# Linear attention and a mixture of experts on one core: rows of the expert pairs gathered by quarters and turned by VectorE

## The chip, the cores and the metric

The kernel runs on one core of one Trainium2 chip. The metric is device time in microseconds, from the first to the last instruction of the launch with what lies around it; the time before is the median of three runs. Engines are TensorE (PE; its weight loads are listed as PEld), VectorE (DVE), ScalarE (ACT), GpSimd (POOL) and SyncE (SP), which issues most transfers.

## The reference

Eight batches of eight heads go through linear attention with exponential features; the result, 4608 rows of 512, goes through a mixture of eight experts, where each row goes to the one expert with the largest gate logit:

```python
def phi(x):
    proj = np.einsum('bhsd,df->bhsf', x, w_phi)
    proj = proj - np.max(np.abs(proj), axis=-1, keepdims=True)
    return np.concatenate([np.exp(proj), np.exp(-proj)], axis=-1)
...
expert_idx = np.argmax(logits, axis=1)
...
gate_w = probs[np.arange(N), expert_idx]
for e in range(E):
    mask = expert_idx == e
    xe = x[mask]
    h = np.maximum(xe @ w1[e], 0.0)
    ye = h @ w2[e]
    out[mask] = gate_w[mask, None] * ye
```

All products keep fp32 accuracy: an operand is split into a high part (rounded to fp32r) and a low part (the rest), and three products (high x high, high x low, low x high) are summed in PSUM.

## The kernel before

**Attention stage** (to about 400 us). Sixteen units of two heads for two batches each. Each unit projects q and k, builds features, sums k features against v, and divides; `normalize` makes rows `xrow`, and `store_rows` writes them to the DRAM table `x_dram`, 128 columns at a time, on SP's queue. A row of `x_dram` has 512 columns and 4 more, in which `gate_store` puts the gate of the row.

**Routing.** While the last attention units run, `route` finds each row's expert and its rank in it. `tokens_of` turns this, with 72 small matmuls into `pp`, into a table `gidx` of 44 blocks of 128 row numbers (gathers) and `sidx` (scatters); `experts_of` finds the expert of each block. Three blocks of the largest expert (`NLEAD`) are known earlier and gathered ahead.

**Expert stage.** Blocks 0 to 37 are worked in 19 pair units of two blocks of one expert (`NPAIR`), the rest as singles (units 19 to 21; more only behind a branch that this input does not take). For each block:
- `gather_rows` (L833) fetches 128 rows of 516 columns into `xg` (4 buffers) with one indirect DMA on GpSimd's queue;
- `x_parts` (L1014 to L1017) turns `xg` with four TensorE transposes into a PSUM tile `px` (2 buffers), ScalarE copies it to the high part `xh`, VectorE subtracts it to the low part `xl` (2 buffers each, a pair unit in one);
- `pair_first` (L1034 to L1042) makes 512 of the unit's hidden values for both blocks in 24 matmuls of 256 columns, four times per unit; ScalarE takes the relu into `hh`, VectorE the rest into `hl`;
- `pair_second` (L1054 to L1056) does twelve matmuls of 512 columns per step into two PSUM tiles `po`, which `write` (L1102, L1104) scales on ScalarE by the gate, column 512 of `xg`, and scatters to the output on GpSimd's queue.

**The order.** The pair loop is written out: per unit u four slots j, each with `pair_first(u, j)`, in slots 2 and 3 `x_parts` of unit u+1, then a `pair_second` step of the slot before; slot 0 calls `gather(u + 1)`, and each slot calls `weights` for two of the eight weight pieces of a later unit. `weights` (L989, L990) casts a raw piece to its high part `wh` on ScalarE and subtracts the low part `wl`, six pieces on VectorE and two (`POOL_LO`, pieces 3 and 7) on GpSimd; raw pieces come over SP's queue, only where the expert changes. This source order gives priorities; a planner then orders each engine's queue from its own estimates of when instructions are ready, within the buffers, and places the waits. `behind` puts an instruction behind another on the same engine.

Of the kernel before, what the change touches and what calls it, by code (L numbers as in the profile page):

```python
# [9 lines left out]
F32 = mybir.dt.float32  # L10
F32R = mybir.dt.float32r
BF16 = mybir.dt.bfloat16
I32 = mybir.dt.int32
# [6 lines left out]
P = 128  # L20
# [25 lines left out]
KD = DM // P  # L46
KF = FF // P
W = 73
XW = DM + 4

WARM = 7
BIG = 8192.0
# [3 lines left out]
def tile_linear_attention_moe(  # L56
# [21 lines left out]
    gidx = keep.tile([P, NB], I32, name="gidx")  # L78
    sidx = keep.tile([P, NB], I32, name="sidx")
    eidx = keep.tile([1, NB], I32, name="eidx")  # L80
    nblk = keep.tile([1, 1], I32, name="nblk")
    gidx0 = keep.tile([P, NLEAD], I32, name="gidx0")
    sidx0 = keep.tile([P, NLEAD], I32, name="sidx0")
# [44 lines left out]
    iota_em = const.tile([P, E], F32, name="iota_em")  # L128
    part_i = const.tile([P, 1], I32, name="part_i")
    part1 = const.tile([P, 1], F32, name="part1")  # L130
    hb_i = const.tile([P, NG, NC], I32, name="hb_i")
    hbase = const.tile([P, NTILE], F32, name="hbase")

# [7 lines left out]
    def constants2():  # L141

        G.memset(ltri, 1.0)
        G.affine_select(ltri, ltri, [[1, P]], ALU.is_gt, 0.0, base=0, channel_multiplier=-1)

        G.iota(iota_i, [[1, P]], base=0, channel_multiplier=0)
        G.tensor_copy(iota_p, iota_i)
        G.tensor_scalar_add(iota_em, iota_e, -float(E))
        G.iota(part_i, [[0, 1]], base=1, channel_multiplier=1)
        G.tensor_copy(part1, part_i)  # L150


        G.iota(hb_i[:, :, 0:4], [[18, NG], [2, 4]], base=0, channel_multiplier=0)
        G.iota(hb_i[:, :, 4:8], [[18, NG], [2, 4]], base=9, channel_multiplier=0)
        G.iota(hb_i[0:64, :, 8:9], [[18, NG], [0, 1]], base=8, channel_multiplier=0)
        G.iota(hb_i[64:P, :, 8:9], [[18, NG], [0, 1]], base=16, channel_multiplier=0)
        G.tensor_copy(hbase, hb_i.rearrange("p g c -> p (g c)"))
        G.tensor_scalar_mul(hbase, hbase, 64.0)
# [8 lines left out]
    bases = [rt.tile([P, E], BF16, name="base0")]  # L167
    V.memset(bases[0], 0.0)

    x_dram = dram.tile([NT, XW], F32, name="x_dram")  # L170


    NPC = KD + KF // 2
# [33 lines left out]
    def col(c):  # L207
        return (0 if c == 8 else P * (c + 1))

    def store_rows(g, t, w0, n, c0=0, nc_=NC, eng=nc.sync):  # L210

        for bb in range(2):
            t0 = (2 * g + bb) * S
            lo, hi = max(c0, 4 * bb), min(c0 + nc_, 4 * bb + 4)
            if lo < hi:
                r0 = t0 + (lo - 4 * bb) * P
                eng.dma_start(
                    x_dram[r0 : r0 + (hi - lo) * P, w0 : w0 + n].rearrange("(c p) w -> p c w", p=P),
                    t[:, lo - c0 : hi - c0, :],
                )  # L220
            if c0 + nc_ == NC:
                nc.sync.dma_start(
                    x_dram[t0 + 4 * P : t0 + S, w0 : w0 + n], t[64 * bb : 64 * bb + 64, 8 - c0, :]
                )

    def load(st, x, part):
# [177 lines left out]
    def num_steps(st, chunks):  # L404


        def step(c, hh, s):
            i = 2 * c + hh
            part = [a <= i < b for a, b in PARTS].index(True)
            a, b = PARTS[part]  # L410
            if (i, s) == (a, 0):
                st["pn"] = ps_nm.tile([P, 7, W], F32, name="pn")
            pn = st["pn"]
            qp, s0 = st["qp", c]
            m = T.matmul(  # L415
                pn[:, i - a, :] if c < 8 else pn[:, 2 + hh : 6 : 2, :],
                qp[:, s, s0 + hh, :],
                st["kf"][:, hh, s, c // 4, :] if c < 8 else st["kf"][:, hh, s],
                start=(s == 0),
                stop=(s == 1),  # L420
            )
            if (i, s) == (b - 1, 1):
                if c == 8:
                    A.copy(pn[D:P, 2:4, :], pn[D:P, 4:6, :])
                normalize(st, a, b, st["pr"])
                if c == 8:
                    lgc_done[st["g"]] += 1
                    eng = G if st["g"] == NG - 1 and st["pr"] == 2 else nc.sync
                    store_rows(st["g"], st["x"], st["pr"] * P, P, eng=eng)
# [194 lines left out]
    def route(g, lgc, c0, n, final=None):  # L624
# [122 lines left out]
            V.tensor_scalar_add(r["se"], r["se"], 1e-9)  # L747

        def gate_store():
            gt = sg.tile([P, NC, XW - DM], F32, name="gt", bufs=2)  # L750
            V.reciprocal(gt[:, 0:n], r["se"].unsqueeze(2).to_broadcast([P, n, XW - DM]))
            store_rows(g, gt, DM, XW - DM, c0, n)

        steps = [logits, top, shift, candidates, first_top, one_hot]
        ranks = [rank, rank_low, rank_high]
# [72 lines left out]

        return [pick_lead, find, find_rows, fetch]

    def gather_rows(index, rows):
        xg = xgp.tile([P, XW], F32, name="xg")
        G.indirect_dma_start(  # L833
            out=xg,
            out_offset=None,
            in_=x_dram[0:rows],
            in_offset=bass.IndirectOffsetOnAxis(ap=index, axis=0),
            bounds_check=rows - 1,
            oob_is_err=False,
        )  # L840
        return xg

    v_tiles = []
    for i in range(2):
# [80 lines left out]
    def tokens_of():  # L925

        pp = ps_kv.tile([P, NB], F32, name="pp", tag="pk")
        for j in range(NTILE):
            T.matmul(pp, sel_p[:, j, :], bsel[:, j, :], start=(j == 0), stop=False)
            T.matmul(pp, sel_h[:, j, :], bsel[:, j, :], start=False, stop=(j == NTILE - 1))  # L930
        V.tensor_scalar(gidx, pp, -1.0, 0.0, op0=ALU.add, op1=ALU.max)
        emp = sg.tile([P, NB], F32, name="emp")
        V.tensor_scalar(emp, pp, 0.5, BIG, op0=ALU.is_lt, op1=ALU.mult)
        st["places"] = V.scalar_tensor_tensor(sidx, pp, -1.0, emp, op0=ALU.add, op1=ALU.add)

    def experts_of():
        ends = sg.tile([1, 2, E], F32, name="ends")
        G.tensor_tensor(ends[:, 0], first[0:1], paired[0:1], op=ALU.add)
        G.tensor_tensor(ends[:, 1], start[0:1], singles[0:1], op=ALU.add)
        V.tensor_reduce(nblk, ends[:, 1], axis=AX.X, op=ALU.max)  # L940
        eg = sg.tile([1, 2, NB, E], F32, name="eg")
        places = ((first[0:1], ends[:, 0], 0, 2 * NPAIR), (start[0:1], ends[:, 1], 2 * NPAIR, NB))
        for low, high, n0, n1 in places:
            for j, edge in enumerate((low, high)):
                m = V.tensor_tensor(
                    eg[:, j, n0:n1],
                    iota_p[0:1, n0:n1].unsqueeze(2).to_broadcast([1, n1 - n0, E]),
                    edge.unsqueeze(1).to_broadcast([1, n1 - n0, E]),
                    op=ALU.is_ge,
                )  # L950
                behind(m, st["places"])
        G.tensor_tensor(eg[:, 0], eg[:, 0], eg[:, 1], op=ALU.subtract)
        G.tensor_tensor(eg[:, 0], eg[:, 0], iota_e[0:1].unsqueeze(1).to_broadcast([1, NB, E]), op=ALU.mult)
# [24 lines left out]
    def weights(u, k):  # L978
# [16 lines left out]
        if u > 0:  # L995
            load_weights(u + 1, k)

    def gather(u):
        if u >= lim[0]:
            return  # L1000
        for b in blocks(u):
            if ("xg", b) not in st:
                st["xg", b] = early_rows[b] if b < NLEAD else gather_rows(gidx[:, b : b + 1], NT)

    def x_parts(u, i):
        if u >= lim[0] or i >= len(blocks(u)) or ("x", u, i) in st:
            return
        if i == 0:
            st["x", u] = [mp.tile([P, KD, 2 * P], F32R, name=n) for n in ("xh", "xl")]
        st["x", u, i] = True  # L1010
        xg = st["xg", blocks(u)[i]]
        px = ps_x.tile([P, KD, P], F32, name="px")
        for k in range(KD):
            T.transpose(px[:, k, :], xg[:, k * P : (k + 1) * P], ident)  # L1014
        xh, xl = (x[:, :, i * P : (i + 1) * P] for x in st["x", u])
        A.copy(xh, px)
        V.tensor_tensor(xl, px, xh, op=ALU.subtract)  # L1017

# [156 lines left out]
    for u in range(1, NPAIR):  # L1175
        for j in range(4):
# [10 lines left out]
    gather(NPAIR + 1)  # L1187
    first_product(NPAIR, 0)
    pair_second(NPAIR - 1, 3)
    weights(NPAIR + 1, 2)  # L1190
# [6 lines left out]
    gather(NPAIR + 2)  # L1197

    def step(u):
        gather(u + 3)  # L1200
        first_product(u + 1, 0)
        h_parts(u, 0)
# [89 lines left out]
```

## Time and profile before

| | |
|---|---|
| median of 3 runs | 902.75 us (902.69 to 902.82) |
| profiled execution, its own time | 900.9 us |
| its span | 899.1 us |
| mean granted TensorE clock | 0.993 of full speed |
| HBM read / written | 128.42 / 20.26 MB |

The span is what the views of the trace cover; times in them are microseconds from its start. A group of the view by lines gives the engine, the operation, the shapes, its count, its busy time in us and the mean of one in ns, and then the idle time of the engine in front of it.

### The profile page before, as it was taken

How to read it: one execution, taken by the hardware profiler on the slowest of the kernel's cores; microseconds unless marked ns; L12 is line 12 of the kernel's file. 1: busy time of each engine (PE TensorE's matmuls, PEld its weight loads, DVE VectorE, ACT ScalarE, POOL GpSimd, SP SyncE). 2: the span in 40 equal slices, each digit the busy share in tenths (PEclk: the TensorE clock that was granted, in tenths of full speed). 3: DMA queues.
4: the chain of work that ended last, by engine and by line, in shares of the span. 5: the costliest groups of instructions: out<-in, count | busy, mean ns of one | idle time of the engine just before them, and what ended most of it. 6: DMA issues, size and time to landing. Idle time of an engine off the chain costs nothing. (4 is left out here: it accounts for less than half of the span.)

```text
span 899.1 us, 18045 instructions
## 1 busy us (share of the span) xinstructions
PE 875.6 (97%) x6767; PEld 825.2 (92%) x6767; DVE 564.6 (63%) x984; ACT 580.4 (65%) x886; POOL 463.0 (51%) x297
## 2 busy tenths in 40 slices
PE   6999999999999999999999999999999999999994
PEld 5999999999999999998899999999999999999883
DVE  6887878877887788759844445544555444444540
ACT  6988888888788888653755555555555555555651
POOL 6777766766677777641533333333333333333341
PEclk9999999999999999999999999999999999999998
DMA  5333333333343333261352243522434634346630
GB/s 158 94 105 100 98 91 93 105 110 109 110 110 100 108 110 80 80 209 19 98 173 71 95 164 118 163 73 77 139 113 146 218 113 146 116 153 223 222 122 15
DMA packets 66795, 106.65 MB, mean 119 GB/s; under 512 B 10830, under 2 KB 28750, under 8 KB 66704
## 3 DMA queue, kind: packets, MB, share of 16 engines
q1 hardware_dynamic: 59312, 84.50, 30.3%
q0 software_dynamic: 6720, 20.80, 7.4%
q8 instruction: 55, 0.90, 0.4%
q14 instruction: 36, 0.29, 0.1%
q10 hardware_dynamic: 672, 0.15, 0.1%
HBM read 128.42 MB, written 20.26 MB: 165 GB/s over the span
## 5 line engine op out<-in xcount | busy, mean ns | idle before, releaser
L990 DVE TENSOR_TENSOR wl<-raw,wh 128x1024 fp32r<-128x1024 f32 x126 | 161.7, 1288 | 144.8 <-ACT wh L989 144.8
L989 ACT CAST wh<-raw 128x1024 fp32r<-128x1024 f32 x168 | 175.1, 1049 | 100.0 <-PE po L1056 71.5
L990 POOL TENSOR_TENSOR wl<-raw,wh 128x1024 fp32r<-128x1024 f32 x42 | 101.4, 2415 | 176.0 <-ACT wh L989 175.7
L415 PE MATMUL pn<-kf,qp 128*128 128x73 f32 (+1 forms) x1152 | 185.0, 255 | 0.0
L1035 PE MATMUL pm<-xl,wh 128*128 128x256 f32 x608 | 172.3, 283 | 0.0
L1036 PE MATMUL pm<-xh,wl 128*128 128x256 f32 x608 | 172.2, 283 | 0.0
L415 PEld LDWEIGHTS pn<-kf,qp 128*128 128x128 f32 x1152 | 171.7, 190 | 0.1
L1034 PE MATMUL pm<-xh,wh 128*128 128x256 f32 x608 | 171.6, 282 | 0.0
L297 POOL TENSOR_TENSOR kl<-e,kh 128x1024 fp32r<-128x1024 f32 x47 | 112.4, 2391 | 102.7 <-ACT kh L295 73.7
L274 DVE TENSOR_REDUCE mx<-ps_proj 128x4 f32<-128x512 f32 (+1 forms) x160 | 101.3, 633 | 58.4 <-PE ps_proj L270 55.4
L1054 PE MATMUL po<-wh,hh 128*128 128x512 f32 x304 | 121.9, 401 | 0.0
L1055 PE MATMUL po<-wl,hh 128*128 128x512 f32 x304 | 119.4, 393 | 0.1
L1035 PEld LDWEIGHTS pm<-xl,wh 128*128 128x128 f32 x608 | 116.4, 191 | 3.0 <-DVE xl L1017 0.2
L1034 PEld LDWEIGHTS pm<-xh,wh 128*128 128x128 f32 x608 | 116.4, 191 | 2.9
L1056 PE MATMUL po<-wh,hl 128*128 128x512 f32 x304 | 118.4, 390 | 0.0
L1036 PEld LDWEIGHTS pm<-xh,wl 128*128 128x128 f32 x608 | 116.4, 191 | 0.0
L359 PE MATMUL pk<-kh,vl 128*64 128x256 f32 x320 | 107.9, 337 | 0.0
L359 PE MATMUL pk<-kh,vh 128*65 128x256 f32 x320 | 105.8, 331 | 1.5 <-ACT kvT L377 1.5
L359 PE MATMUL pk<-kl,vh 128*65 128x256 f32 x320 | 106.2, 332 | 0.8 <-DVE kl L297 0.8
L275 DVE TENSOR_TENSOR t<-ps_proj,mx 128x512 f32<-128x512 f32 (+1 forms) x160 | 101.5, 635 | 4.6
L240 POOL TENSOR_TENSOR xl<-xr,xh 128x512 fp32r<-128x512 f32 (+2 forms) x63 | 101.5, 1629 | 2.5 <-ACT xh L239 2.4
L1042 DVE SCALAR_TENSOR_TENSOR hl<-pm,hh 128x512 fp32r<-128x512 f32 x76 | 52.2, 687 | 69.0 <-ACT hh L1041 69.0
(206 smaller groups left out, 1875.0 us busy)
## 6 DMA issues: line engine op xcount, KB each, us to landing
raw<-w SPq DMA_DIRECT2D x168, 512.0 KB
vt<-vv SPq DMA_DIRECT2D x15, 640.0 KB
x_dram<-xrow SPq DMA_DIRECT2D x30, 256.0 KB
xr<-kT SPq DMA_DIRECT2D x15, 320.0 KB
xr<-qT SPq DMA_DIRECT2D x15, 320.0 KB
xr<-kT SPq DMA_DIRECT2D x17, 256.0 KB
xr<-qT SPq DMA_DIRECT2D x17, 256.0 KB
x_dram<-xrow SPq DMA_DIRECT2D x32, 32.0 KB
```

What stands on the lines that cost most here:

```text
L240: el.tensor_tensor(xl[:, 0:n], xr[:, 0:n], xh[:, 0:n], op=ALU.subtract)
L297: eng.tensor_tensor(kl, e[:, 0:m], kh, op=ALU.subtract)
L359: return T.matmul(st["pk", bb][0:n, hh, :], (vl if j == 1 else vh)[:, 2 * (c + (bb if c == 8 else 0)) + hh, 0:n], (kl if j == 2 else kh)[: ...
L415: m = T.matmul(pn[:, i - a, :] if c < 8 else pn[:, 2 + hh : 6 : 2, :], qp[:, s, s0 + hh, :], st["kf"][:, hh, s, c // 4, :] if c < 8 else s ...
L989: A.copy(th, raw[k])
L990: m = (G if k in (POOL_LO if u else POOL_LO0) else V).tensor_tensor(tl, raw[k], th, op=ALU.subtract)
L1034: T.matmul(pm[:, i], th, xh[:, k, :], start=(k == 0), stop=False)
L1035: T.matmul(pm[:, i], th, xl[:, k, :], start=False, stop=False)
L1036: T.matmul(pm[:, i], tl, xh[:, k, :], start=False, stop=(k == KD - 1))
L1054: T.matmul(po, hh[:, i, r], th[:, c], start=(i == j == 0), stop=False)
L1055: T.matmul(po, hh[:, i, r], tl[:, c], start=False, stop=False)
L1056: T.matmul(po, hl[:, i, r], th[:, c], start=False, stop=(i == 1 and j == 3))
```

## The change

- In units 4 to 18 (`by_quarters`) each block is fetched by four indirect DMAs. The table `x_dram` has rows of exactly 512 columns now and is read as 4 x 4608 quarter rows of 128 columns. DMA c puts, on partition 32q + t, quarter q of row 32c + t of the block. The quarter numbers, 4 x row + q, come from `quarters_of`: four fp32 matmuls spread the row numbers over the partitions, one VectorE instruction makes the integers `qidx`.
- Such a block is turned by one VectorE transpose of 32x32 squares into `px`, in place of four TensorE transposes. On partition p then lie columns 4p to 4p+3. The rows of w1 are put into that order on the host, and the transposes that stay on TensorE read every fourth column.
- Gates go to a table `g_dram` of 4 columns; `gather_gates` fetches them per block with an indirect DMA of their own into `gate` (6 buffers), and `write` scales by that.
- Rows are gathered two units ahead instead of one (`gather(u + 2)`); gates one unit ahead. `gather(2)` and the first gates stand before the loop, behind the arithmetic of `experts_of`.
- In units 1 to 18 VectorE does all eight low-part subtractions of the weights; in unit 0 and the singles GpSimd keeps two.

```diff
-XW = DM + 4
+XW = 4
+Q = P // 4
...
+        for q in range(4):
+            G.memset(quad[q * Q : (q + 1) * Q], float(q))
...
-    x_dram = dram.tile([NT, XW], F32, name="x_dram")
+    x_dram = dram.tile([NT, DM], F32, name="x_dram")
+    g_dram = dram.tile([NT, XW], F32, name="g_dram")
...
-            store_rows(g, gt, DM, XW - DM, c0, n)
+            store_rows(g, gt, g_dram, 0, XW, c0, n)
...
+    def gather_quarters(b):
+        xg = xgp.tile([P, 4, P], F32, name="xg")
+        quarters = x_dram.rearrange("t (q d) -> (t q) d", q=4)
+        for c in range(4):
+            behind(fetch_rows(xg[:, c, :], quarters, qidx[:, c, b : b + 1], 4 * NT), st["experts"])
+        return xg
+
+    def gather_gates(b):
+        gate = xgp.tile([P, XW], F32, name="gate", bufs=6)
+        index = gidx0[:, b : b + 1] if b < NLEAD else gidx[:, b : b + 1]
+        return gate, fetch_rows(gate, g_dram, index, NT)
...
+    def quarters_of():
+        spread = raw2.tile([P, 4, P], F32, name="spread")
+        G.tensor_copy(
+            spread.rearrange("p c (i t) -> p c i t", i=4),
+            ident.rearrange("p (c t) -> p c t", c=4).unsqueeze(2).to_broadcast([P, 4, 4, Q]),
+        )
+        pq = ps_kv.tile([P, 4, NB], F32, name="pq", tag="pk")
+        for c in range(4):
+            T.matmul(pq[:, c, :], spread[:, c], st["rows"], start=True, stop=True)
+        V.tensor_scalar(qidx, pq, 4.0, quad, op0=ALU.mult, op1=ALU.add)
...
-        m = (G if k in (POOL_LO if u else POOL_LO0) else V).tensor_tensor(tl, raw[k], th, op=ALU.subtract)
+        m = (G if k in (POOL_LO0 if u == 0 else POOL_LO if u >= NPAIR else ()) else V).tensor_tensor(tl, raw[k], th, op=ALU.subtract)
...
+    def by_quarters(u):
+        return 4 <= u < NPAIR
...
-        for k in range(KD):
-            T.transpose(px[:, k, :], xg[:, k * P : (k + 1) * P], ident)
         xh, xl = (x[:, :, i * P : (i + 1) * P] for x in st["x", u])
+        if by_quarters(u):
+            px = px.rearrange("p c (k t) -> p c k t", t=Q)
+            V.transpose(px, xg.rearrange("p c (d k) -> p c k d", k=KD))
+            px = px.rearrange("p c k t -> p k c t")
+            xh, xl = (x.rearrange("p k (c t) -> p k c t", t=Q) for x in (xh, xl))
+        else:
+            for k in range(KD):
+                T.transpose(px[:, k, :], xg.rearrange("p c d -> p (c d)")[:, k : DM : KD], ident)
...
-        A.activation(ob, po, AF.Copy, scale=st["xg", b][:, DM : DM + 1])
+        A.activation(ob, po, AF.Copy, scale=st["gate", b][:, 0:1])
...
     experts_of()
+    quarters_of()
+    gates(0)
+    gather(2)
+    gates(1)
...
             if j == 0:
-                gather(u + 1)
+                gather(u + 2)
+                gates(u + 1)
```

## Rows read from the trace of the kernel before

**Rows 1.** The page's table of engines: busy time, share of the span, instructions.
```profile
PE 875.6 (97%) x6767; PEld 825.2 (92%) x6767; DVE 564.6 (63%) x984; ACT 580.4 (65%) x886; POOL 463.0 (51%) x297
```

**Rows 2.** Windows of the pair loop: length, busy us by engine, clock, DMA, GB/s.
```profile
core 0: us, PE busy (x) PEld busy (x) DVE busy (x) ACT busy (x) POOL busy (x), PEclk, DMA share, GB/s
437.00:460.00 23.00, 23.00 (x152) 21.04 (x151) 17.06 (x16) 16.04 (x20) 9.37 (x5) 1.00 0.40 137
...
600.00:693.00 93.00, 93.00 (x607) 85.15 (x606) 44.67 (x49) 49.95 (x65) 36.17 (x24) 1.00 0.36 118
```

**Rows 3.** Timeline of PE, one pair unit: start, duration (us), instruction.
```profile
602.61 0.28 PE L1034 MATMUL pm<-xh,wh 128*128 128x256 f32 x1
...
605.48 0.60 PE L1014 MATMUL px<-ident,xg 128*128 128x128 f32 x4
...
608.67 0.28 PE L1034 MATMUL pm<-xh,wh 128*128 128x256 f32 x1
...
614.72 0.28 PE L1034 MATMUL pm<-xh,wh 128*128 128x256 f32 x1
...
620.34 0.28 PE L1034 MATMUL pm<-xh,wh 128*128 128x256 f32 x1
...
625.96 0.28 PE L1034 MATMUL pm<-xh,wh 128*128 128x256 f32 x1
```

**Rows 4.** Groups by line: transposes of the whole span; VectorE from 490 to 860 us.
```profile
L1014 PE MATMUL px<-ident,xg 128*128 128x128 f32 x164 | 24.6, 272 | 0.8 <-DMA xg<-x_dram,gidx 0.8
...
L990 DVE TENSOR_TENSOR wl<-raw,wh 128x1024 fp32r<-128x1024 f32 x97 | 122.2, 1261 | 128.2 <-ACT wh L989 128.2
...
L1017 DVE TENSOR_TENSOR xl<-px,xh 128x512 fp32r<-128x512 f32 x32 | 21.8, 681 | 0.0
```

**Rows 5.** Timeline of GpSimd, one pair unit; in brackets the idle time before.
```profile
504.06 1.02 POOL L1104 DMA_INDIRECT out<-ob,sidx  x1 [4.45 <-ACT ob L1102]
505.39 1.04 POOL L833 DMA_INDIRECT xg<-x_dram,gidx  x1 [0.30 <-issue]
...
508.06 1.03 POOL L1104 DMA_INDIRECT out<-ob,sidx  x1 [0.30 <-issue]
...
527.41 1.02 POOL L1104 DMA_INDIRECT out<-ob,sidx  x1 [4.46 <-ACT ob L1102]
```

**Rows 6.** Timelines of GpSimd and VectorE: two gathers beside subtractions.
```profile
433.53 2.01 POOL L833 DMA_INDIRECT xg<-x_dram,gidx  x1 [0.31 <-ACT wh L989]
...
600.15 1.01 POOL L833 DMA_INDIRECT xg<-x_dram,gidx  x1 [0.30 <-issue]
...
432.30 2.36 DVE L990 TENSOR_TENSOR wl<-raw,wh 128x1024 fp32r<-128x1024 f32 x2 [1.65 <-ACT wh L989]
...
600.31 1.23 DVE L990 TENSOR_TENSOR wl<-raw,wh 128x1024 fp32r<-128x1024 f32 x1 [0.18 <-ACT wh L989]
```

**Rows 7.** Groups by line and form, VectorE: a copy and a strided reduction.
```profile
L397 DVE COPY kf<-pf 128x292 f32<-128x292 f32 x32 | 14.5, 453 | 3.3 <-PE pf L386 3.3
...
L645 DVE TENSOR_REDUCE pt<-lgc 128x72 f32<-128x576 f32 x3 | 3.8, 1251 | 0.9 <-PE ps_proj L269 0.9
```

**Rows 8.** Timelines of ScalarE and VectorE around 611 us.
```profile
610.90 1.05 ACT L989 CAST wh<-raw 128x1024 fp32r<-128x1024 f32 x1 [0.98 <-PE pm L1035]
...
613.12 0.68 DVE L1042 SCALAR_TENSOR_TENSOR hl<-pm,hh 128x512 fp32r<-128x512 f32 x1
613.73 0.68 DVE L1017 TENSOR_TENSOR xl<-px,xh 128x512 fp32r<-128x512 f32 x1
```

**Rows 9.** Timelines before the pair loop, and one group by line.
```profile
428.65 0.65 PE L1014 MATMUL px<-ident,xg 128*128 128x128 f32 x4 [0.82 <-DMA xg<-x_dram,gidx]
...
428.45 0.92 POOL L953 TENSOR_TENSOR eg<-eg,iota_p 1x352 f32<-1x352 f32 x1
...
L386 PE MATMUL pf<-fold,kvT 65*128 65x73 f32 x256 | 40.5, 252 | 0.0
```

**Rows 10.** Instructions on the tile xg: transfer time, in us from issue.
```profile
DMA to landing us min/median/max: 3.5/3.6/3.7
```

More of the change, by code (lines that the diff above doesn't have):

```diff
@@ L80, in tile_linear_attention_moe @@
     eidx = keep.tile([1, NB], I32, name="eidx")
+    qidx = keep.tile([P, 4, NB], I32, name="qidx")
     nblk = keep.tile([1, 1], I32, name="nblk")
@@ L130, in tile_linear_attention_moe @@
     part1 = const.tile([P, 1], F32, name="part1")
+    quad = const.tile([P, 1], F32, name="quad")
     hb_i = const.tile([P, NG, NC], I32, name="hb_i")
@@ L208, in col, with store_rows @@
         return (0 if c == 8 else P * (c + 1))
-    def store_rows(g, t, w0, n, c0=0, nc_=NC, eng=nc.sync):
+    def store_rows(g, t, rows, w0, n, c0=0, nc_=NC, eng=nc.sync):
         for bb in range(2):
@@ L217, in store_rows @@
                 eng.dma_start(
-                    x_dram[r0 : r0 + (hi - lo) * P, w0 : w0 + n].rearrange("(c p) w -> p c w", p=P),
+                    rows[r0 : r0 + (hi - lo) * P, w0 : w0 + n].rearrange("(c p) w -> p c w", p=P),
                     t[:, lo - c0 : hi - c0, :],
@@ L222, in store_rows @@
                 nc.sync.dma_start(
-                    x_dram[t0 + 4 * P : t0 + S, w0 : w0 + n], t[64 * bb : 64 * bb + 64, 8 - c0, :]
+                    rows[t0 + 4 * P : t0 + S, w0 : w0 + n], t[64 * bb : 64 * bb + 64, 8 - c0, :]
                 )
@@ L428, in step @@
                     eng = G if st["g"] == NG - 1 and st["pr"] == 2 else nc.sync
-                    store_rows(st["g"], st["x"], st["pr"] * P, P, eng=eng)
+                    store_rows(st["g"], st["x"], x_dram, st["pr"] * P, P, eng=eng)
             return m
@@ L749, in gate_store @@
         def gate_store():
-            gt = sg.tile([P, NC, XW - DM], F32, name="gt", bufs=2)
-            V.reciprocal(gt[:, 0:n], r["se"].unsqueeze(2).to_broadcast([P, n, XW - DM]))
-            store_rows(g, gt, DM, XW - DM, c0, n)
+            gt = sg.tile([P, NC, XW], F32, name="gt", bufs=2)
+            V.reciprocal(gt[:, 0:n], r["se"].unsqueeze(2).to_broadcast([P, n, XW]))
+            store_rows(g, gt, g_dram, 0, XW, c0, n)
         steps = [logits, top, shift, candidates, first_top, one_hot]
@@ L829, in lead, with fetch_rows @@
         return [pick_lead, find, find_rows, fetch]
[L831 to L834, printed above, removed]
+    def fetch_rows(out, source, index, rows):
+        return G.indirect_dma_start(
+            out=out,
             out_offset=None,
-            in_=x_dram[0:rows],
+            in_=source[0:rows],
             in_offset=bass.IndirectOffsetOnAxis(ap=index, axis=0),
@@ L840, in gather_rows @@
         )
-        return xg
+    def gather_rows(index, rows):
+        xg = xgp.tile([P, 4, P], F32, name="xg")
+        fetch_rows(xg.rearrange("p q d -> p (q d)"), x_dram, index, rows)
+        return xg
+    def gather_quarters(b):
+        xg = xgp.tile([P, 4, P], F32, name="xg")
+        quarters = x_dram.rearrange("t (q d) -> (t q) d", q=4)
[6 more added lines that the diff above has]
+        return gate, fetch_rows(gate, g_dram, index, NT)
     v_tiles = []
@@ L934, in tokens_of @@
         st["places"] = V.scalar_tensor_tensor(sidx, pp, -1.0, emp, op0=ALU.add, op1=ALU.add)
+        st["rows"] = sg.tile([P, NB], F32, name="rows_f")
+        V.tensor_scalar(st["rows"], pp, -1.0, 0.0, op0=ALU.add, op1=ALU.max)
+    def quarters_of():
[6 more added lines that the diff above has]
+        for c in range(4):
+            T.matmul(
+                pq[:, c, :],
+                spread[:, c],
+                st["rows"],
+                start=True,
+                stop=True,
+            )
+        V.tensor_scalar(qidx, pq, 4.0, quad, op0=ALU.mult, op1=ALU.add)
     def experts_of():
@@ L952, in experts_of @@
         G.tensor_tensor(eg[:, 0], eg[:, 0], eg[:, 1], op=ALU.subtract)
-        G.tensor_tensor(eg[:, 0], eg[:, 0], iota_e[0:1].unsqueeze(1).to_broadcast([1, NB, E]), op=ALU.mult)
+        st["experts"] = G.tensor_tensor(eg[:, 0], eg[:, 0], iota_e[0:1].unsqueeze(1).to_broadcast([1, NB, E]), op=ALU.mult)
         with nc.allow_low_precision("experts are integers"):
@@ L1002, in gather, with gates @@
             if ("xg", b) not in st:
-                st["xg", b] = early_rows[b] if b < NLEAD else gather_rows(gidx[:, b : b + 1], NT)
+                if b < NLEAD:
+                    st["xg", b] = early_rows[b]
+                elif by_quarters(u):
+                    st["xg", b] = gather_quarters(b)
+                else:
+                    st["xg", b] = gather_rows(gidx[:, b : b + 1], NT)
+    def gates(u):
+        if u < lim[0]:
+            for b in blocks(u):
+                if ("gate", b) not in st:
+                    st["gate", b], m = gather_gates(b)
+                    behind(m, st["experts"])
     def x_parts(u, i):
@@ L1012, in x_parts @@
         px = ps_x.tile([P, KD, P], F32, name="px")
-        for k in range(KD):
-            T.transpose(px[:, k, :], xg[:, k * P : (k + 1) * P], ident)
         xh, xl = (x[:, :, i * P : (i + 1) * P] for x in st["x", u])
+        if by_quarters(u):
[3 more added lines that the diff above has]
+            xh, xl = (x.rearrange("p k (c t) -> p k c t", t=Q) for x in (xh, xl))
+        else:
+            for k in range(KD):
+                T.transpose(px[:, k, :], xg.rearrange("p c d -> p (c d)")[:, k : DM : KD], ident)
         A.copy(xh, px)
@@ L1182, in tile_linear_attention_moe @@
             if j == 0:
-                gather(u + 1)
+                gather(u + 2)
+                gates(u + 1)
             for du, k in AHEAD_W[j]:
                 weights(u + du, k)
-    gather(NPAIR + 1)
     first_product(NPAIR, 0)
@@ L1199, in step @@
     def step(u):
+        gates(u)
         gather(u + 3)
@@ L1259, in blocks, with shuffled @@
         return res
+    def shuffled(w):
+        return np.ascontiguousarray(w.reshape(E, P, KD, FF).transpose(0, 2, 1, 3).reshape(E, DM, FF))
     def rows(a):
@@ L1278 @@
         "w_gate": np.ascontiguousarray(inputs["moe_w_gate"]),
-        "w1": np.ascontiguousarray(inputs["moe_w1"]),
+        "w1": shuffled(np.asarray(inputs["moe_w1"])),
         "w2": np.ascontiguousarray(inputs["moe_w2"]),
```

## Prediction, made before the change was run

> **What bounds the kernel now.** I read the page's table of engines first, then the windows, then single timelines. TensorE is busy 97% of the span [rows 1]. The windows say where that share is a limit: from 437 us on, in the pair loop, PE is busy in every microsecond of each window, at a granted clock of 1.00 (the 2.4 GHz level), while VectorE has 44.67, ScalarE 49.95 and GpSimd 36.17 of 93 us [rows 2]. So in this stage a microsecond is won only by what leaves PE's queue, and the other engines may take on work until one of them is full or hands something over late.
>
> The PE timeline gives the length of one pair unit. Starts of the four first products of a unit: 602.61, 608.67, 614.72, 620.34, and the next unit at 625.96 [rows 3]. The two slots in which a block's rows are turned (four transposes each, the row at 605.48 is one set) last 6.06 and 6.05 us, the two without them 5.62 each: 23.35 us in all. The GpSimd timeline shows the same period, 504.06 to 527.41 [rows 5].
>
> **The removed transposes.** The blocks of units 4 to 18 are turned one unit earlier, in loop units 3 to 17: 15 units, 30 blocks, 120 of the 164 transposes. A slot without them is (6.06 + 6.05 − 2 × 5.62) / 2 = 0.435 us shorter. That is the price to use, not the 272 ns of one transpose [rows 4], which overlaps its neighbours. 30 × 0.435 = 13.1 us; a unit falls to 22.48 us. This is the first term: −13.1.
>
> **VectorE.** Per unit it works 44.67 / 93 × 23.35 = 11.2 us [rows 2]. The change adds two low-part subtractions that GpSimd did in the pair loop (1.26 us each [rows 4]) and two turns of 128x512. No row shows a turn. From below it is bounded by the copy of 292 columns, 0.45 us, from above by the strided reduction of 576 columns, 1.25 us [rows 7]; I take 0.7, near the 0.68 of xl, which moves the same 512 columns [rows 4]. Sum: 11.2 + 2.5 + 1.4 = 15.1 us of 22.48 (16.2 at 1.25). VectorE has the room, so the term is nothing as long as its results are in time; cover is 6 to 7 us a unit. The Trainium skill, "VectorE: DVE Perf Modes", section "The three transpose paths", gives 311 ns for a 128x128 bf16 turn on VectorE; four of them would be an estimate of 1.24 us, and the sum would be the same.
>
> **Is a turned block in time?** Today the order is tight: hl at 613.12 and xl at 613.73 for a unit whose first product starts at 614.72 [rows 3, 8]. If the turn stood in VectorE's queue behind hl, then turn 0.7, xh 0.58 and xl 0.68 would end near 613.81 + 1.96 = 615.8; without the transposes PE wants it at 614.72 − 0.435 + 0.12 = 614.4. But a turn needs nothing from PE, and the queues don't run in source order: two out scatters stand before the two gathers in the source, yet one scatter goes out behind them [rows 5]; and the cast at 610.90 starts exactly when PE's last read frees its buffer, about half a unit before its place in the source, ahead of the hh of the slot [rows 8]. Work is issued as early as buffers allow. The buffers (4 for xg, 2 for px, 2 for xh and xl) let a block be gathered two units and turned one unit before use. So I cost the new chain at nothing, with 1.4 us a unit as the other bound.
>
> **GpSimd.** A unit now has 8 quarter gathers, 2 gate gathers and 2 scatters instead of 2 gathers and 2 scatters, and loses two subtractions. Issues follow each other every 1.33 us [rows 5]: 12 × 1.33 = 16.0 of 22.48 us. One row warns: the gather at 433.53 took 2.01 us, begun inside a pair of VectorE subtractions that ran from 432.30 to 434.66; the one at 600.15, begun before the subtraction at 600.31, took 1.01 [rows 6]. So an issue that starts inside such a subtraction may wait for its end. Eight subtractions a unit can each hold up one issue by at most their own 1.26 us: 16.0 to 26.1 us; half of that wait gives 21.0, still under 22.48. A gather lands 3.6 us after issue [rows 10] and has more than a unit of lead. I take nothing. The Trainium skill, "SBUF — State Buffer", section "Who interferes with whom", says that a VectorE instruction with two SBUF inputs shuts out a GpSimd instruction that reads SBUF, whichever comes second waiting for the other's end. The trace agrees, with 2.01 against 1.01 us, and a rival below stands on that row.
>
> **The change-over to the pair loop.** Four fp32 matmuls build the quarter indices: by 40.5 us / 256 = 0.16 us of PE for a small fp32 matmul [rows 9] that is 0.6 us, some of it inside the 0.82 us that PE already waits for a gather at 428.65 [rows 9]. The gates of the first unit are gathered only behind the expert arithmetic, which ends at 428.45 + 0.92 = 429.4: they land at 433.0 and 434.3 [rows 5, 10], and the scaling that frees the PSUM tiles ends near 435.0. The second product that reuses one comes at least two first products (2.87 us each, 602.61 to 605.48 [rows 3]) after 428.65, so at 434.4 or later: 0 to 0.6 us. In the first pair units VectorE was busiest, 17.06 of 23 us [rows 2], and gets about 2.5 us more per unit; hl has a slot of 5.6 us to spare, so 0 to 1 us. The 44 transposes that stay read every fourth column: no row shows what that costs, 0 to 2 us if each set took 0.2 longer; I take nothing. From these 0 to 4.2 us I take 0.6.
>
> **SP, the loads, the end.** Rows of 2048 instead of 2064 bytes and gates in a table of their own keep the number of transfers in the attention stage. The same bytes are gathered in the pair loop, in four times as many pieces. The singles behind the loop keep their transposes and their split of work: nothing.
>
> **Sum.** −13.1 + 0.6 = −12.5 us. The profiled execution is 900.9 us (span 899.1), 1.85 under the median of 902.75; 900.9 − 12.5 = 888.4, and with the same offset **890.3 us**. Its own range, with all the open costs of the change-over, is 889 to 894.
>
> **Rivals.**
> - *Partly late.* The turned rows come in time in most units, but VectorE or a late gather holds PE by some 0.3 to 0.6 us in the others: 30 blocks at 0.15 to 0.3 is 4.5 to 9 us given back, 895 to 899. For it: VectorE gets 15 to 16 us of ordered work in 22.5. Against: a unit of lead.
> - *The new chain takes the place of the transposes, slower.* If the turn is issued behind hl after all, PE waits 1.4 us at each of 15 unit starts for xl: −13.1 + 21 + 0.6 = +8.5, 911 us. It decides from 0.87 us a unit on, where the wait eats the gain. For it: the source order and today's 1 us between xl and its use; against: the cast at 610.90 [rows 8].
> - *GpSimd becomes the bound, slower.* The wait of the row at 433.53 [rows 6] at every subtraction gives 26.1 us a unit: 15 × (26.1 − 23.35) = +41, 944 us. It decides when an issue takes 23.35 / 12 = 1.95 us on average with its gap. For it: 2.01 in one row; against: 1.0 in most.
> - *No change.* Something else keeps the old pace of 23.35 us (casts, loads), and PE only idles where it turned rows: 902.75 + 0.6. Against it: ScalarE has 12.5 of 23.35 us and its casts wait for PE's reads, not the other way round [rows 2, 8].
>
> **Chances.** Forecast 0.67; partly late 0.13; new chain 0.08; GpSimd 0.07; no change 0.05. A change of about 0.2% (1.8 us) is what a measurement here can tell from none. The first two are faster, the last is the same: faster 0.80, same 0.05, slower 0.15. The 8 in 10 range holds the first two: 888.0 (a transpose worth slightly more than I read, no cost in the change-over) to 899.0.
>
> **What would show it.** Right: 44 transposes left on PE; slots of 5.6 us throughout loop units 3 to 17; windows with PE full; 30 turns on VectorE of 0.5 to 1.25 us; GpSimd at some 16 to 21 us a unit, its gathers a unit ahead. Wrong: idle time on PE or its weight loads ended by VectorE's xl (second rival), by a DMA into xg or a gather waiting on GpSimd (third), indirect gathers near 2 us, or an idle stretch of several microseconds around 425 to 440 us, where the gates and the indices are new.

## The result, and the profile after

The changed kernel takes 895.0 us (median of 12 runs, 891.3 to 898.6) against 902.8 us (12 runs, 900.9 to 905.7) of the kernel before beside it: a ratio of 0.991 with an interval of 0.989 to 0.993, 7.8 us faster. The forecast of 890.3 us is missed by 4.7; the range of 888 to 899 holds the time. The profiled execution took 895.85 us, its span 894.1 against 899.1 us. Every kernel here, the one before too, scatters by some us from run to run, and two traces below (GpSimd keeps its pieces; the plain turn again) come from runs at the slow end of their kernel: they are read for what happens in them, not for their time.

The page's table of engines, in answer to [rows 1]:

```profile
PE 867.1 (97%) x6655; PEld 814.7 (91%) x6655; DVE 626.2 (70%) x1050; ACT 580.3 (65%) x886; POOL 554.6 (62%) x399
```

TensorE lost 8.5 us of busy time, VectorE and GpSimd gained 62 and 92. First products of the four slots of unit 4 on the PE timeline, with the start of unit 5, in answer to [rows 3], and the groups on the tile `px` (ns min/median/max):

```profile
506.95 0.28 PE L1099 MATMUL pm<-xh,wh 128*128 128x256 f32 x1
...
512.57 0.28 PE L1099 MATMUL pm<-xh,wh 128*128 128x256 f32 x1
...
518.19 0.28 PE L1099 MATMUL pm<-xh,wh 128*128 128x256 f32 x1
...
523.81 0.28 PE L1099 MATMUL pm<-xh,wh 128*128 128x256 f32 x1
...
529.43 0.28 PE L1099 MATMUL pm<-xh,wh 128*128 128x256 f32 x1
```
```profile
L1080 PE MATMUL px<-ident,xg x44: 270/285/421, 393.5 to 862.2; 128*128 128x128 f32 x44
...
L1075 DVE STREAM_TRANSPOSE px<-xg x30: 1061/1106/1168, 480.8 to 783.2; 128x512 f32<-128x512 f32 x30
```

All four slots last 5.62 us, a unit 22.48: the loop is what was forecast to a hundredth. VectorE's queue shows why no turned block is late:

```profile
619.92 0.68 DVE L1082 TENSOR_TENSOR xl<-px,xh 128x512 fp32r<-128x512 f32 x1
...
621.78 0.68 DVE L1082 TENSOR_TENSOR xl<-px,xh 128x512 fp32r<-128x512 f32 x1
622.38 1.11 DVE L1075 STREAM_TRANSPOSE px<-xg 128x512 f32<-128x512 f32 x1
623.39 0.67 DVE L1107 SCALAR_TENSOR_TENSOR hl<-pm,hh 128x512 fp32r<-128x512 f32 x1
623.98 1.06 DVE L1075 STREAM_TRANSPOSE px<-xg 128x512 f32<-128x512 f32 x1
```

As soon as `xl` has read `px`, the turn of the next unit goes in, a unit ahead and partly before `hl`. The windows show where the time went that the loop had won, in answer to [rows 2] (same columns):

```profile
437.00:460.00 23.00, 18.51 (x93) 15.71 (x94) 14.97 (x15) 15.43 (x20) 16.27 (x14) 0.85 0.14 43
460.00:483.00 23.00, 22.03 (x146) 19.96 (x145) 15.56 (x18) 12.67 (x17) 12.80 (x11) 1.00 0.60 199
600.00:693.00 93.00, 92.57 (x588) 84.16 (x587) 60.38 (x63) 51.31 (x66) 56.08 (x48) 1.00 0.35 107
```

From 437 to 460 us PE was busy 18.51 of 23 us where it had been full, and the granted clock was 0.85, so part of the window was at the lower of the two levels (1.2 GHz). Three timelines of that place, GpSimd, ScalarE and PE (and last, a line of PE in the kernel before):

```profile
424.40 1.11 POOL L838 DMA_INDIRECT xg<-x_dram,gidx  x1 [5.98 <-DVE emp L956]
425.81 1.18 POOL L838 DMA_INDIRECT xg<-x_dram,gidx  x1 [0.30 <-issue]
...
428.60 1.00 POOL L838 DMA_INDIRECT xg<-x_dram,gidx  x1 [0.30 <-issue]
...
431.76 0.94 POOL L997 TENSOR_TENSOR eg<-eg,iota_p 1x352 f32<-1x352 f32 x1
432.86 1.04 POOL L838 DMA_INDIRECT gate<-g_dram,gidx  x1 [0.16 <-issue]
```
```profile
435.28 0.69 ACT L1167 ACTIVATE ob<-po,gate 128x512 f32<-128x512 f32 x1 [6.03 <-DMA gate<-g_dram,gidx]
436.64 0.69 ACT L1167 ACTIVATE ob<-po,gate 128x512 f32<-128x512 f32 x1 [0.68 <-DMA gate<-g_dram,gidx]
437.23 1.98 ACT L1033 CAST wh<-raw 128x1024 fp32r<-128x1024 f32 x2
439.11 0.60 ACT L1106 ACTIVATE hh<-pm 128x512 fp32r<-128x512 f32 x1
```
```profile
427.88 0.75 PE L1080 MATMUL px<-ident,xg 128*128 128x128 f32 x4 [0.48 <-DMA xg<-x_dram,gidx]
...
435.77 0.29 PE L1080 MATMUL px<-ident,xg 128*128 128x128 f32 x1
439.76 0.79 PE L1119 MATMUL po<-wh,hh 128*128 128x512 f32 x1 [3.70 <-ACT wh L1033]
440.35 0.63 PE L1120 MATMUL po<-wl,hh 128*128 128x512 f32 x1
...
459.63 0.39 PE L1099 MATMUL pm<-xh,wh 128*128 128x256 f32 x1 [1.60 <-ACT xh L1081]
...
461.45 0.39 PE L1100 MATMUL pm<-xl,wh 128*128 128x256 f32 x1 [0.97 <-DVE xl L1082]
```
```profile
497.95 0.28 PE L1034 MATMUL pm<-xh,wh 128*128 128x256 f32 x1
```

Read upwards: PE stands still for 3.70 us until the `hh` of 439.11 is there at 439.71 (the row names ScalarE's weight cast, the instruction behind it); `hh` stands in ScalarE's queue behind two output copies `ob` and two weight casts, and the first copy waited 6.03 us for its gate; the gate was issued at 432.86, since the planner had put the four row gathers of units 2 and 3 in front (with the one of unit 1, which came first before too, five from 424.40 to 431.7, and only after the fourth and fifth the two expert instructions). Until 445.5 us PE then ran at the lower clock, 0.43 us from one matmul of 512 columns to the next in place of 0.23, and it paused twice more, 2.57 us together.

The first product of unit 4 starts at 506.95 us, before at 497.95. Two turns are already saved there (0.87), so the change-over lost 9.9 us. Counted from the end of PE's wait for the first gathered row, at 427.88 and before at 428.65 [rows 9], it is 79.07 against 69.30 us, a loss of 10.6. TensorE's last matmul ends 1.3 us earlier than before (886.2 against 887.5), and the span ends 5.0 us earlier: the stretch behind the last matmul was 11.6 us and is 7.9.

### The profile page after: what moved, and what is told of

Read it like the earlier page. It is cut to its first block, busy times and chain, and to the rows that moved or that the text cites. A ratio compares the mean times of both kernels' runs of the same rounds, so it can differ in the third digit from the quotient of the medians.

```text
span 894.1 us, 18171 instructions
## 1 busy us (share of the span) xinstructions
PE 867.1 (97%) x6655; PEld 814.7 (91%) x6655; DVE 626.2 (70%) x1050; ACT 580.3 (65%) x886; POOL 554.6 (62%) x399
## 5 line engine op out<-in xcount | busy, mean ns | idle before, releaser
L1034 DVE TENSOR_TENSOR wl<-raw,wh 128x1024 fp32r<-128x1024 f32 x160 | 195.9, 1234 | 116.2 <-ACT wh L1033 76.0
L838 POOL DMA_INDIRECT xg<-x_dram,qidx x120 | 150.7, 1256 | 72.6 <-DVE px L1075 33.3
L274 PE MATMUL ps_proj<-w_hi,xh 128*128 128x256 f32 x288 | 83.4, 290 | 5.8 <-DVE t L281 5.8
```

What stands on the lines that cost most here:

```text
L838: return G.indirect_dma_start(out=out, out_offset=None, in_=source[0:rows], in_offset=bass.IndirectOffsetOnAxis(ap=index, axis=0), bounds_ ...
L1034: m = (G if k in (POOL_LO0 if u == 0 else POOL_LO if u >= NPAIR else ()) else V).tensor_tensor(tl, raw[k], th, op=ALU.subtract)
```

## Experiments

Each ran beside the kernel before on the same chip; its median was 902.3 us in the first four, 903.7 in the next four and 903.5 in the last three.

**1. Lead gates early.** The gates of the three blocks known ahead are fetched behind their rows.

```diff
             for i in range(NLEAD):
                 early_rows.append(gather_rows(gidx0[:, i : i + 1], NEARLY * P))
+            for i in range(NLEAD):
+                gate = xgp.tile([P, XW], F32, name="gate", bufs=6)
+                fetch_rows(gate, g_dram, gidx0[:, i : i + 1], NEARLY * P)
+                early_gates.append(gate)
```

> The changed kernel, but the gates of the three blocks whose rows are fetched early are fetched with those rows, so the first two output copies of ScalarE have their gates long before they run; the order of the other GpSimd work is that of the changed kernel. Theory A (the time lost at the change-over is mainly ScalarE held by the first output copy, which waits for a gate that GpSimd fetches behind five row gathers): the copy at 435.28 us no longer waits, TensorE's pause of 3.70 us at 439.76 goes, and with it most of the stretch of slow matmuls after it, 6 to 7 us together; the two pauses at 459.6 and 461.5 us (2.6 us) stay, since the expert indices stay late: 888 to 890 us. Theory B (the loss comes from the expert indices alone, and the held ScalarE is beside the path): no change, 895 us. Theory C (the loss is not at the change-over but in the loop or the tail): no change.

Measured: 887.7 us, ratio 0.983 (0.980 to 0.985). The window of the change-over and GpSimd's last expert instruction:

```profile
437.00:460.00 23.00, 22.86 (x148) 20.65 (x147) 20.36 (x21) 17.00 (x22) 19.04 (x14) 1.00 0.28 88
```
```profile
435.09 0.94 POOL L1001 TENSOR_TENSOR eg<-eg,iota_p 1x352 f32<-1x352 f32 x1
```

PE has no pause worth naming after 432 us, and the clock stays at 1.00. The expert indices are as late as in the changed kernel (the instruction ends 8.3 us after the start of the first row gather in both: 427.73 to 436.03, and 424.40 to 432.70). Theory B falls, and so does a part of theory A as written: the two later pauses were not the indices' doing, they went with the held ScalarE.

**2. Gates first.** `behind` puts the whole-row gathers of unit 2 and after behind the last gate gather of unit 0.

```diff
-                    st["xg", b] = gather_rows(gidx[:, b : b + 1], NT)
+                    st["xg", b] = gather_rows(gidx[:, b : b + 1], NT, st.get("gates0"))
```

> The changed kernel with GpSimd's order put right and nothing fetched earlier than it was: the gathers of whole rows of the third unit and after come behind the two gate gathers of the first unit, and these come straight behind the expert work. Theory A and B both expect the expert indices back at about 429.5 us and the two pauses at 459.6 and 461.5 us gone; the first gate lands at about 433 us instead of 435.3, so about 2.3 us of TensorE's 3.70 us pause goes and perhaps the slow stretch behind it: 886 to 890 us. Theory C: no change, 895 us.

Measured: 887.1 us, ratio 0.983 (0.981 to 0.986). ScalarE's copies again:

```profile
434.25 1.27 ACT L1171 ACTIVATE ob<-po,gate 128x512 f32<-128x512 f32 x2 [3.17 <-DMA gate<-g_dram,gidx]
```

`ob` still waits 3.17 us for its gate, and PE pauses 0.19 and 0.59 us: half the wait costs PE almost nothing.

**3. Both.** Lead gates early, and `behind(..., st["experts"])` for the whole-row gathers.

> The changed kernel with both: the three lead gates fetched with the early rows, and the whole-row gathers of the third unit and after behind the expert work. If the change-over is where the loss is (theories A and B), the whole of it comes back, and the time is that of the kernel before less the 13.1 us of the turns taken from TensorE, plus up to 1 us for the index matmuls: 888 us by the median, in any case 3 us or more below each of the two repairs alone if they are separate losses, or equal to the better of them if the two pauses are one loss. Theory C: 895 us.

Measured: 886.6 us, ratio 0.981 (0.979 to 0.984), no pause of PE after 432 us. It is equal to the better of the two repairs within the scatter, so there was one loss and not two. From the end of the wait for the first gathered row to the first product of unit 4, experiments 1, 2 and 3 take 69.22, 70.17 and 68.82 us, where the kernel before took 69.30 and the changed one 79.07.

**4. The gain alone.** The kernel before without the turns.

```diff
+        if 4 <= u < NPAIR:
+            px = xg[:, 0:DM].rearrange("p (k t) -> p k t", k=KD)
+        else:
+            px = ps_x.tile([P, KD, P], F32, name="px")
             for k in range(KD):
                 T.transpose(px[:, k, :], xg[:, k * P : (k + 1) * P], ident)
```

> The kernel before, with the turns left out in units 4 to 18: the rows go into the two halves of the input as they were gathered, not turned, so the output of those blocks is not the reference's. It measures the gain alone, without the gate table, the quarter gathers and the new order of the loop. By the term of the prediction, 30 blocks by 0.435 us: 13.1 us less than the kernel before, 889.7 us, with steps of 5.62 us in the loop in place of 6.06 and 5.62. If the four turns of a block hide behind something else in the loop, less than 13 us; if the tail takes up part of what the loop gives, the end of TensorE moves by 13 us and the time by less.

Measured: 889.8 us, ratio 0.987 (0.985 to 0.989), 12.5 us less than before. The first product of the third slot of unit 1 and the last matmul, here and in the kernel before:

```profile
439.66 0.28 PE L1037 MATMUL pm<-xh,wh 128*128 128x256 f32 x1
...
874.64 0.39 PE L1099 MATMUL po<-wh,hl 128*128 128x512 f32 x1
```
```profile
439.06 0.28 PE L1034 MATMUL pm<-xh,wh 128*128 128x256 f32 x1
...
887.12 0.39 PE L1096 MATMUL po<-wh,hl 128*128 128x512 f32 x1
```

PE takes 434.98 us from one to the other, before 448.06: 13.1 less. The stretch behind the last matmul stays at 11.6 us.

**5. Gate table without quarters.** `by_quarters` returns False, GpSimd keeps its pieces; all else as in the changed kernel.

> The changed kernel with whole rows in every unit: TensorE turns all of them as before and GpSimd keeps its two weight pieces, so what is left of the change is the gate table, the gathers one unit further ahead, the order of GpSimd's queue at the change-over, the index matmuls and the strided reads of TensorE's transposes. If the loss at the change-over is all of the difference between the gain of the turns (12.5 us in the kernel without turns) and the gain of the whole change (7.8 us), and the end of the run is no different from the kernel before: 9 us slower than before, 911 us. If the shorter end that every kernel with the gate table showed so far (8 us from the last matmul to the end of the span in place of 11.6) comes from the gate gathers: 3.6 us less, 907 to 908 us, with TensorE's end some 9 us later than before in both cases. If the strided transposes cost more than the plain ones, the slots with turns are longer than 6.06 us.

Measured: 911.8 us, ratio 1.011 (1.007 to 1.014), 8.1 us slower, as with a loss of 9 us or more and a shorter end: in its trace the end takes 7.5 us. The strided transposes have a price:

```profile
641.25 0.28 PE L1099 MATMUL pm<-xh,wh 128*128 128x256 f32 x1
...
647.37 0.28 PE L1099 MATMUL pm<-xh,wh 128*128 128x256 f32 x1
```

A slot with one set lasts 6.12 us, not the 6.06 and 6.05 of [rows 3]. That is 0.065 us a set, 2.7 us for the 41 sets here and 0.7 for the 11 that the changed kernel has left; an estimate of what the new order itself costs is then 8.1 + 4.1 − 2.7 = 9.5 us, from the medians, the shorter end (11.6 − 7.5) and the sets. PE pauses here as in the changed kernel, 3.48 us before the matmul at 439.20.

**6. GpSimd keeps pieces 3 and 7.** Experiment 3 with the split of the kernel before.

```diff
-        m = (G if k in (POOL_LO0 if u == 0 else POOL_LO if u >= NPAIR else ()) else V).tensor_tensor(tl, raw[k], th, op=ALU.subtract)
+        m = (G if k in (POOL_LO if u else POOL_LO0) else V).tensor_tensor(tl, raw[k], th, op=ALU.subtract)
```

> The repaired kernel (lead gates early, experts first), but GpSimd keeps its two weight pieces per unit in the pair loop, as in the kernel before, beside the twelve gathers and scatters. This doses the rival that GpSimd becomes the bound. By the issues measured in the repaired kernel's steady loop (62 us busy in 93 us, with 0.3 us behind each of about twelve issues: 18.6 us a unit) plus 2 x 2.4 us, GpSimd needs 23.4 us of a unit of 22.48 us: it falls behind by about 1 us a unit once its lead is used up, up to 14 us over the loop, 890 to 901 us. If the issues alone count at 1.33 us each (16.0 + 4.8 = 20.8 us), it has room and the time is that of the repaired kernel, 887 us. VectorE's turns get shorter only if its two fewer weight pieces matter to GpSimd's issues.

Measured: four runs of 905.9, 925.2, 927.8 and 930.1 us. The fastest is 19.3 us above experiment 3 and above both expectations; a price cannot be read from so wide a spread. A window of the loop in the run of 927.8 us, and VectorE's group of subtractions:

```profile
600.00:693.00 93.00, 88.60 (x548) 77.44 (x547) 55.22 (x52) 45.77 (x60) 69.84 (x54) 1.00 0.34 105
```
```profile
L1040 DVE TENSOR_TENSOR wl<-raw,wh 128x1024 fp32r<-128x1024 f32 x126 | 181.7, 1458 | 102.4 <-ACT wh L1039 71.4 <-issue 31.0
```

GpSimd is at work or between two issues (0.3 us each) for some 86 of 93 us, VectorE's subtraction takes 1.46 us in place of 1.24, PE waits for `hl`, which VectorE makes, ten times in the loop, and stretches of slow issue (below) come on top. How much each takes was not separated, and that GpSimd itself is the bound here is not shown. But a loop in which PE waits is only two subtractions away.

**7. Plain turn.** Experiment 3 with the turn reading runs of 32 numbers, the transposes plain columns.

```diff
-            V.transpose(px, xg.rearrange("p c (d k) -> p c k d", k=KD))
+            V.transpose(px, xg.rearrange("p c (k d) -> p c k d", k=KD))
```

> The repaired kernel with VectorE's turn reading plain runs of 32 numbers in place of every fourth one, and TensorE's transposes in the other units reading plain columns again; the host orders the first weights for the turned units, so the blocks of the other units are not the reference's. Theory A (the fourfold stride of the read sets the turn's 1.10 us): the turn falls to about 0.7 us, the price that the prediction took. Theory B (the instruction has its price whatever the stride): it stays at 1.06 to 1.17 us. The time is that of the repaired kernel in both cases, 887 us, because VectorE has a third of each unit idle and turns a unit ahead; if TensorE's strided transposes cost anything, its slots with turns (three units) get shorter by that.

Measured: 895.1 us, ratio 0.991 (0.988 to 0.994). The turn, in ns:

```profile
L1081 DVE STREAM_TRANSPOSE px<-xg x30: 681/717/726, 481.9 to 782.2; 128x512 f32<-128x512 f32 x30
```

Without the stride of the read, the 1.10 us of the turn become 0.72. The Trainium skill, "VectorE: DVE Perf Modes", section "The three transpose paths", led to an estimate of 1.24 us for a turn of this size; the two rows, 1.10 and 0.72, are both below it. The time was a miss: the steps of the loop are 5.62 us again, and TensorE lost 7.5 us against experiment 3 between 440 and 456 us, before any turn had run.

**8. More quarters.** Experiment 3 with `by_quarters` from unit 2 on, singles included (`return u >= 2`).

> The repaired kernel with quarter rows from the third unit on and in the single blocks at the end as well: two more units of pairs and three single blocks lose their turns on TensorE, 7 blocks by 0.435 us, so 3.0 us less than the repaired kernel, 883.5 us, if GpSimd still has each gate in time: at the change-over it has sixteen more issues of 1.33 us in its queue before the gates of the second unit. If those come late, ScalarE is held at the first output copies of the second unit, as in the changed kernel, and the time is 3 to 6 us more than the repaired kernel's, 890 to 893 us.

Measured: 909.8 us, ratio 1.007 (1.005 to 1.009); both expectations missed. No output copy waits for a gate. From 443 to 473 us TensorE issues slowly, as in experiment 7 but longer.

**9 and 10. Experiments 3 and 7 again, on one chip.**

> The repaired kernel (lead gates early, experts first) once more, beside the kernel with the plain turn, on one chip. The plain-turn kernel has the same instructions in the same order on every engine and was 8.5 us slower, with slow stretches of TensorE at 443 to 455 us before any turn of VectorE had run. Theory A (the two edits of the plain turn cost that): the repaired kernel again gives 886 to 888 us here and the plain-turn kernel 895 us. Theory B (the change-over of either kernel can fall into such a stretch, and which does is a matter of the chip or of the run): both give the same, near 887 or near 895 us, or both scatter between the two.

> The plain-turn kernel once more, beside the repaired kernel on the same chip; the blocks of the units that TensorE still turns are not the reference's. Theory A: 895 us again, 8 us above the repaired kernel. Theory B: the time of the repaired kernel beside it, and where a run is slow, the slow stretch stands at the change-over again while the steps of the loop stay at 5.62 us.

Measured: 888.6 us (886.6 to 894.1), ratio 0.986 (0.983 to 0.990), and 888.8 us (887.3 to 901.1), ratio 0.986 (0.982 to 0.989). The two are equal and both scatter: theory B. In the trace of the second (the run of 901.1 us), such a stretch lies in the loop, not at the change-over as theory B had it:

```profile
503.73 0.38 PE L1106 MATMUL pm<-xl,wh 128*128 128x256 f32 x1 [0.43 <-issue]
...
505.15 0.28 PE L1105 MATMUL pm<-xh,wh 128*128 128x256 f32 x1 [0.92 <-issue]
...
506.57 0.28 PE L1106 MATMUL pm<-xl,wh 128*128 128x256 f32 x1 [0.79 <-issue]
...
508.00 0.28 PE L1107 MATMUL pm<-xh,wl 128*128 128x256 f32 x1 [0.81 <-issue]
```

A few matmuls, then 0.8 to 0.9 us of nothing, every 1.43 us; ScalarE and VectorE wait for PE meanwhile. The slot took 16.5 us (503.0 to 519.5) in place of 5.62, the later part of it at the lower clock (0.69 granted over the slot).

**11. The end.** The kernel before with a gather of 16-byte rows for each block, into a tile that nothing reads.

```diff
+                if b >= NLEAD:
+                    tiny = xgp.tile([P, 4], F32, name="tiny")
+                    G.indirect_dma_start(
+                        out=tiny,
...
+                        in_=x_dram.rearrange("t (g f) -> (t g) f", f=4)[0:NT],
...
```

> The kernel before, with one more gather of 16-byte rows for each block behind its row gather, into a tile that nothing reads; the rows stay 516 numbers wide and the gate stays in them. It asks where the shorter end of all kernels with the gate table comes from (11.6 us from the last matmul to the end of the span before, 7.5 to 8.0 us with the table). If the count of GpSimd's transfers sets it: 8 us here as well and 3 to 4 us less than before, 899 us. If the width of the rows or the table itself sets it: 11.6 us, and 903 us. If GpSimd's added 2.7 us a unit hold up scatters and row gathers at the change-over, up to 3 us more on TensorE's side.

Measured: 935.8 us, ratio 1.036 (1.034 to 1.039). The time missed every expectation: since nothing waits for these gathers, the planner put all 38 into the change-over (GpSimd's timeline from 425 to 493 us). PE waited twice:

```profile
461.55 0.58 PE L1044 MATMUL pm<-xh,wh 128*128 128x256 f32 x1 [10.03 <-ACT xh L1026]
...
498.31 1.11 PE L1024 MATMUL px<-ident,xg 128*128 128x128 f32 x4 [18.34 <-DMA xg<-x_dram,gidx]
```

The longer wait is for rows gathered behind the small gathers. The shorter is for an `xh` that stood in ScalarE's queue behind weight casts, and these had waited 11.36 us for a raw piece; GpSimd's own subtraction of a piece stood among the gathers, at 454.68 us. The loop after 506 us is as before. But its end answers the question: 7.4 us (923.0 to 930.4). GpSimd's last drain, the longest of three, in ns, in the kernel before, the changed kernel, experiment 4 and this one:

```profile
L1288 POOLq DRAIN  x3: 40/107/6939, 891.3 to 898.8; - x3
```
```profile
L1362 POOLq DRAIN  x3: 40/107/732, 892.6 to 893.9; - x3
```
```profile
L1291 POOLq DRAIN  x3: 40/107/6939, 878.8 to 886.3; - x3
```
```profile
L1298 POOLq DRAIN  x3: 40/107/1794, 927.8 to 930.1; - x3
```

## Why the prediction was right or wrong

- **What bounds the kernel, and the removed transposes (−13.1): right.** Experiment 4 gives 13.1 us of TensorE's time and 12.5 us of the median; in the changed kernel all slots of the loop are 5.62 us.
- **VectorE (nothing): right, with a wrong duration.** The turn takes 1.10 us where 0.7 was taken, inside the stated bounds of 0.45 and 1.25; VectorE is busy 60 to 64 of 93 us in the loop. A plain turn (0.72) moves no step of the loop.
- **The turned block in time (nothing): right.** The turn is issued when its buffer comes free, as read from the cast at 610.90 [rows 8]. The loop has no wait for `xl`.
- **GpSimd (nothing): right, near its edge.** In experiment 3 it is busy 61.98 of 93 us; with 0.3 us behind each of twelve issues that is 15.0 + 3.6 = 18.6 us a unit, between the two bounds of 16 and 26 and near the 21 that half the wait gave. With the 4.8 us a unit of two subtractions added, experiment 6, TensorE waits in the loop, though not shown to be for GpSimd.
- **The change-over (+0.6, at most 4.2): wrong; this is the step that failed.** It cost 9.9 us in the trace (10.6 from the first gathered row on), some 9.5 by experiment 5, and 7 to 8 by the medians with and without the repair (experiments 3 and 9). The mechanism was named (gates behind the expert arithmetic, an output copy behind the gates), but the arithmetic was taken to end at 429.4 as before. The four row gathers that the planner moves ahead of it were not counted, though the change moves `gather(2)` ahead; they put the issue of the first gate at 432.9. (It then landed in 2.4 us, at 435.3, and not in the 3.6 that a row takes.) And the price was set by the PSUM tiles that the copy frees, not by what stands behind the copy in ScalarE's queue: two weight casts and the next `hh`, without which TensorE has nothing to do. The second copy ended at 437.33; TensorE went on at 439.76, with `hh`. The lower clock after the pause and two later pauses came on top. Experiments 1 and 2, one with earlier gates and the other with their order alone put right, give back about 7 us each.
- **The strided transposes (taken as nothing, bound 2): 0.7 us.** The index matmuls take 0.8 us of PE's queue (424.85 to 425.67) where 0.6 was taken, but PE's wait for the first gather fell to 0.48 from 0.82 us [rows 9], so about 0.5 is left of them.
- **The end (not in the sum): −3.7 us.** Nothing in the prediction looked behind the last matmul. GpSimd's last drain, the instruction that ends its queue, shrinks from 6.94 to 0.73 us; experiment 11 shows that more gathers alone shorten it. Why is open. Part of it is given back: the last scatter goes out at 889.44 us, 3.23 behind the end of the last matmul in place of 1.00, with no wait that the profile names.
- **Slow issue (not in the sum).** The changed kernel's trace has 1.0 us of it (three waits at 690 and 755 us); other runs have more. It may be part of the scatter of 7 us. So may TensorE's clock ahead of the change-over: from 375 to 400 us it was granted at 1.00 in the traces of both kernels and of experiments 5, 6 and 11 and at 0.86 to 0.93 in the others, and PE's wait for the first gathered row ended at 427.5 to 429.3 us in the first and 429.3 to 433.2 in the second.

Put together: 12.5 off for the turns by the medians, 3.7 off for the end by the traces, and 7.8 off measured, so 8.4 were lost; the change-over and the strided transposes stand for them. Two errors of opposite sign, the change-over and the end, brought the time just above the forecast's own range of 889 to 894 and to the rival "partly late", 895 to 899, by another way than that rival's: no turned row is late. That the wide range holds the time is in part luck. Without the change-over, experiment 3, the same change is 15.7 us faster than before by its first measurement and 15.0 by its second, faster than both kernels.

## What to carry to other kernels

A transfer that is split from another one (a gate from its row) is a new place in an in-order queue: list what the planner can put in front of it, and what stands behind its reader, at the one place in the program where the queue is full, before the steady loop is looked at. The price of a late operand is not what its reader frees but everything behind the reader on its engine. And count the tail: of the 5.0 us by which the span became shorter in the two traces, 3.7 lie behind the last matmul.

## What was not expected of the hardware

- GpSimd's drain at the end takes 6.94 us in two kernels (the one before and experiment 4) and 0.73 to 2.45 us in all that issue more gathers, whatever their rows.
- TensorE can fall into stretches of 4 to 30 us where it issues a few matmuls and then pauses, for 0.2 to 1.6 us (once 2.1), with nothing in the profile that it waits for, at either clock. They stand in the traces of experiments 6, 7, 8 and 10, where GpSimd issues gathers back to back, with single pauses in the changed kernel and experiment 9, and in none of the kernel before or of experiments 1 to 4; but in the loop of experiment 3, and from 425 to 493 us in experiment 11, GpSimd is as dense without them. The cause is open.
- A 128x512 fp32 turn on VectorE takes 0.72 us from plain runs and 1.10 us when it reads every fourth number; on TensorE the weight load of such a transpose takes 0.21 us in place of 0.14.
